# Attention and a tanh-shrink layer in one hand-ordered kernel: turns 96 to 574 of the first quarter in another order, 28 operations on another engine

## The chip, the cores and the metric

One Trainium2 core. It has TensorE (PE; matmuls into PSUM, with a weight load, PEld, ahead of each), VectorE (DVE), ScalarE (ACT), GpSimd (POOL) and SyncE (SP, which here only issues transfers). The metric is the device time of one execution in microseconds (us); the median of the runs is compared. PSUM has eight banks of 128 partitions by 2 KB; a matmul writes into them, and the other engines read the result out.

## The reference

Inputs q, k, v of [8 batches, 8 heads, 576 positions, 64] in float32 and two weights, w_in [512, 2048] and w_out [2048, 512]. The attention is a sum of two softmax attentions:

```python
# pooled: means over groups of 4 positions, result repeated 4 times
out_d = sm_attn(q_d, k_d, v_d);  out_up = np.repeat(out_d, 4, axis=2)
# local: only keys with |i - j| < 4
scores = np.where(np.abs(i - j) < 4, scale * q @ k.T, -1e9)
attn_out = out_up + softmax(scores) @ v
# the layer, on 4608 tokens of 512 values
x = attn_out.transpose(0, 2, 1, 3).reshape(4608, 512)
h = x @ w_in
out = (h - np.tanh(h)) @ w_out
```

## The kernel before, in words

**Pairs and batches.** Two heads make a pair, p = 0 to 31, four pairs make a batch, b = 0 to 7. A batch is one block of 576 tokens of the layer, so the attention of batch b is followed by the layer of block b, and attention for the next batch runs between the matmuls of the layer. The change lies in the stretch in which batch 0 and 1 (pairs 0 to 7) go through attention, the beginning of pair 8, and block 0's first layer.

**One pair, step by step, with lines.** SP issues the loads of q and k (tile st, 512 positions) and v (vst, 160 KB a head). The last 64 positions of all four pairs of a batch come as one tile sr, once a batch. Then:

- casts to bf16: qr for k and for q (L545, two operations), vw for v (L471), and once a batch rr from sr (L535). L535, L545 and L471 can each run on DVE, ACT or POOL.
- for pairs 0 to 7, PE transposes qr (L552) into PSUM, four transposes for k and four for q; kt (L557) and kq (L562) are copies of these out of PSUM, by ACT or DVE. Once a batch PE transposes rr (L575), ACT copies that to rT (L579), and the last columns of kt (L607) and kq (L612) are copied from rT. Later pairs use transposes by DMA that SP issues.
- the pooled k and q (qkd): for pairs 0 to 3, sums by PE (L659, L662) and a copy (L667); later, adds by DVE or POOL (L644 and L648 into half, L638 into qkd).
- scores in two parts, the first L696, the second L706 and L712. ACT takes the exp of the first part (L717) and of the second (L721 local, L725 pooled) into E; E is multiplied by the mask (L752, DVE or POOL).
- pooled v: PE (L502, from vw and the constant pick), copied into vp by ACT or DVE (L506). Its remainder, vpr, is built once a batch by three adds and multiplications (L433 vrs, L437 vrp, L440 vpr).
- the outs (L766), 18 matmuls of E with vw, vp and vpr; DVE takes the reciprocal r of the sums (L782) and multiplies (L784, tile ln).
- PE transposes ln back (L809, six transposes); od is a copy of the pooled part (L813 ACT, L815 DVE), and DVE joins both parts into xT, the layer's input (L802).

**The layer.** The first matmul of block 0 (L843) writes h for 128 of the 2048 columns in four steps, one for each pair's xT. ACT takes the tanh (L855) into u and DVE subtracts (L858) into gT. The second layer is L1137 and L1279; its results are copied to y (L1151 DVE or ACT). POOL issues the loads of the weights: w_in in four quarters (L452) and w_out in four (L456). Some filler matmuls of 128 by 512 (L1519), 24 in all, are placed by a string (FILL) where PE would otherwise be idle; they compute nothing that is used.

**The order is written out by hand.** The class Plan records 2263 operations with what each reads and writes, and emits them in the order of the string TURNS, two characters a turn. Each engine so gets its instructions in a fixed order, and an instruction that waits holds up all behind it on that engine. ENGINES has a letter for each operation that has a choice of engine (A for ACT, D for DVE, P for POOL). BANKS has a digit for each operation that opens PSUM banks; it can open them when everything that uses their earlier holder is done. BEHIND has pairs of operations: the first waits until the second is done, with the reason "shared port in this order". A wait from data, from a bank or from BEHIND becomes a semaphore wait.

```python
for i in turn:
    fn, deps, opens, names = self.ops[i]
    ...
    for name, sets in opens:
        c = self.place[name] = sets[int(next(seats))]
        ...
    if fn is not None:
        fn()
        ...
        if i in before:
            tc.add_manual_dep(seen[0], last[before[i]], ...)
```

## Time and profile before

| | before |
|---|---|
| median of 3 runs (us) | 308.03 (307.83 to 308.14) |
| profiled execution: its time, its span (us) | 311.41, 309.70 |
| TensorE, busy | 297.1 us, 96% |
| VectorE, busy | 266.9 us, 86% |
| ScalarE, busy | 224.3 us, 72% |
| GpSimd, busy | 157.1 us, 51% |
| granted clock of TensorE, mean | 0.992 |

The times are given by the slowest core, of which there is one here. The profile is of a single execution, whose time of 311.41 us stands beside the runs' median of 308.03; its span of 309.70 goes from its first recorded instruction to the last. In the profile, busy shares are of the span; a row of the timeline gives the start, the duration, the engine, the line and what the engine waited for before it (in brackets, with the time and the instruction that ended the wait). A row of windows gives busy time of each engine in a stretch, then the clock that was granted to TensorE (1.00 is full speed), the mean busy share of the DMA engines and what they moved in GB/s. In the page's rows of slices, each digit is a fortieth of the span, 7.7 us, in tenths.

Matmuls overlap: a row's duration includes a tail that runs on while the next matmul has started. What a step takes of TensorE when another follows at once is the distance from its start to the next start, called its slot here.

### The profile page before, as it was taken

The page shows a single profiled execution, that of the slowest core. Times are in us where ns is not written, and L with a number is a line of the kernel's source. Part 1 is how long each engine was busy: PE and PEld are TensorE (multiplying, and loading weights), DVE is VectorE, ACT ScalarE, POOL GpSimd, SP SyncE. Part 2 cuts the span into 40 slices and gives each one's busy share as a digit, 9 for nine tenths or more (in the row PEclk, how much of TensorE's full clock was granted, in tenths as well). Part 3 has the DMA queues.
Part 4 walks back from the last instruction along what each step waited for, and adds up shares of the span by engine and source line. Part 5 has one row for each costly group of instructions (what it writes and reads, how often), then busy time and mean ns, then how long its engine had stood idle before and what let it go on. Part 6 is the DMA issues. An engine that isn't in the chain of part 4 may idle for free.

```text
span 309.7 us, 8119 instructions
## 1 busy us (share of the span) xinstructions
PE 297.1 (96%) x3100; PEld 211.3 (68%) x3100; DVE 266.9 (86%) x493; ACT 224.3 (72%) x403; POOL 157.1 (51%) x213
## 2 busy tenths in 40 slices
PE   7777999999999999999999999999999999999994
PEld 3556555645487765784577755655988888889983
DVE  2674899688998988899998899899999999998783
ACT  3657678359887786888967888899867898875300
POOL 5325766108665546338874258547424264616550
PEclk9997999999999999999999999999999999999998
DMA  7999999989999999969999999999989526000333
GB/s 227 234 242 247 244 229 142 193 211 261 241 247 270 219 238 230 311 145 236 233 262 198 296 220 200 245 226 236 206 214 242 145 28 186 2 3 2 135 122 85
DMA packets 121191, 60.83 MB, mean 196 GB/s; under 512 B 88896, under 2 KB 119104, under 8 KB 121152
## 3 DMA queue, kind: packets, MB, share of 16 engines
q1 hardware_dynamic: 115968, 55.27, 76.9%
q0 software_dynamic: 4224, 4.19, 8.5%
q10 hardware_dynamic: 960, 0.85, 1.0%
q8 instruction: 24, 0.39, 0.5%
q14 instruction: 15, 0.12, 0.1%
HBM read 44.04 MB, written 9.44 MB: 173 GB/s over the span
## 4 chain that ended last, share of the span: by engine, by line
PE 87%; DMA 4%; SPq 3%; DVE 3%; issue 1%; ACT 1%; ACTq 0%
PE ps L1279 27%; PE ps L843 26%; PE ps L953 8%; PE ps L766 5%; PE ps L991 5%; PE ps L1137 4%; PE ps L696 3%; PE ps L1109 2%; SPq L411 2%; PE ps L1076 2%; DMA st<-in_k_dram 2%; DMA sr<-in_k_dram 2%; PE ps L809 1%; PE ps L712 1%; PE ps L502 1%; SPq L387 1%
## 5 line engine op out<-in xcount | busy, mean ns | idle before, releaser
L843 PE MATMUL ps<-xT,w_in_sb 128*128 128x512 bf16 x384 | 91.5, 379 | 0.0
L1279 PEld LDWEIGHTS <-gT 128*128 128x128 bf16 x672 | 64.5, 98 | 12.3
L858 DVE TENSOR_TENSOR gT<-ps,u 128x512 bf16<-128x512 f32 x96 | 64.2, 684 | 6.8 <-ACT u L855 5.6
L855 ACT ACTIVATE u<-ps 128x512 f32<-128x512 f32 x96 | 56.4, 599 | 16.3 <-PE ps L843 14.5
L843 PEld LDWEIGHTS <-w_in_sb 128*128 128x128 bf16 x384 | 35.3, 98 | 35.7
L545 POOL CAST qr<-st 128x512 bf16<-128x512 f32 x42 | 25.3, 613 | 42.2 <-DVE Tw L1188 15.5
L1279 PE MATMUL ps<-w_out_sb,gT 128*128 128x256 bf16 x336 | 43.4, 273 | 0.0
L1279 PE MATMUL ps<-Tw,gT 128*128 128x256 bf16 x336 | 42.5, 273 | 0.0
L717 ACT ACTIVATE E<-ps 128x912 bf16<-128x912 f32 x32 | 29.8, 932 | 6.3 <-PE ps L706 5.8
L784 DVE TENSOR_TENSOR ln<-ps,r 128x768 bf16<-128x768 f32 x32 | 30.6, 955 | 0.8
L623 ACT COPY kt<-kq 128x576 bf16<-128x576 bf16 x23 | 27.2, 1184 | 0.8 <-DMA kq<-qr 0.5
L766 PEld LDWEIGHTS <-E 128*128 128x128 bf16 x576 | 21.9, 98 | 6.0 <-DVE E L752 1.4
L752 DVE TENSOR_TENSOR E<-E,mask 128x1152 bf16<-128x1152 bf16 x31 | 23.5, 759 | 1.9 <-ACT E L721 1.6
L633 POOL TENSOR_TENSOR half<-kq 128x576 f32<-128x576 bf16 x16 | 20.5, 1278 | 8.4 <-ACT u L855 3.5
L725 ACT ACTIVATE E<-ps 128x576 bf16<-128x576 f32 x32 | 20.9, 654 | 1.4 <-PE ps L712 1.4
L766 PE MATMUL ps<-vw,E 128*128 128x65 bf16 x320 | 19.2, 194 | 1.0 <-DVE E L752 0.6
L638 POOL TENSOR_TENSOR qkd<-half 128x288 bf16<-128x288 f32 x21 | 16.7, 796 | 5.8 <-DVE r L782 2.0
L1214 DVE TENSOR_TENSOR gT<-gT 128x2048 bf16<-128x2048 bf16 x14 | 17.3, 1233 | 0.2
L1365 POOL TENSOR_TENSOR y<-y,keep 128x512 f32<-128x512 f32 x8 | 10.2, 1275 | 13.4 <-DVE E L752 4.8
L991 PE MATMUL ps<-xT,w_in_sb 128*128 128x128 bf16 x256 | 16.8, 219 | 0.0
L471 ACT CAST vw<-vst 128x640 bf16<-128x640 f32 x22 | 15.7, 729 | 1.1 <-DMA vst<-in_v_dram 1.1
L1301 ACT COPY y<-ps 128x512 f32<-128x512 f32 x19 | 11.1, 587 | 7.5 <-PE ps L1279 6.7
(183 smaller groups left out, 598.6 us busy)
## 6 DMA issues: line engine op xcount, KB each, us to landing
vst<-in_v_dram SPq DMA_DIRECT2D x56, 160.0 KB, 4.3
st<-in_q_dram SPq DMA_DIRECT2D x28, 256.0 KB, 4.1
st<-in_k_dram SPq DMA_DIRECT2D x28, 256.0 KB, 5.2
out_dram<-y SPq DMA_DIRECT2D x14, 512.0 KB, 4.2
v<-in_v_dram SPq DMA_DIRECT2D x20, 256.0 KB, 3.1
w_in_sb<-in_moe_w_in_dram POOLq DMA_DIRECT2D x4, 512.0 KB, 8.4
w_out_sb<-in_moe_w_out_dram POOLq DMA_DIRECT2D x4, 512.0 KB, 7.0
vr<-in_v_dram SPq DMA_DIRECT2D x8, 128.0 KB
```

What stands on the lines that cost most here:

```text
L545: (eng, ns, lambda dst=dst, src=src, fn=fn: fn(out=dst, in_=src), port)
L623: ("ACT", 1180, lambda: A.copy(out=ktv, in_=src), False),
L717: A.activation(out=E[s][:, :, E0:E0 + 456], in_=at(s1)[:, :, PS0:512], func=AF.Exp, scale=SCALE)
L752: eng.tensor_tensor(out=el, in0=el, in1=mask.unsqueeze(1).to_broadcast([128, 2, S]), op=ALU.mult)
L766: T.matmul(po[:, hh, 65 * n:65 * n + 65], E[s][:, hh, e:e + 128], vv, start=start, stop=stop)
L784: op("DVE", 960, lambda: V.tensor_tensor(out=ln[s].rearrange("p n (h d) -> p h n d", d=D), in0=blocks()[:, :, :, 0:64], in1=r[s].unsqueeze ...
L843: T.matmul(at(name)[:, 0, :], w_in_sb[:, dc, fc * 128:(fc + 1) * 128], xT[dc][:, c0:c0 + S].rearrange("p (c g) -> p c g", c=4)[:, :, 0:128 ...
L855: op("ACT", 600, lambda: A.activation(out=u[us], in_=at(name)[:, 0, :], func=AF.Tanh), reads=[("hd", kb, fc)], writes=[("u", us)], uses=[n ...
L858: op("DVE", 690, lambda: V.tensor_tensor(out=gT[g][:, fc, :], in0=at(name)[:, 0, :], in1=u[us], op=ALU.subtract), reads=[("hd", kb, fc), ( ...
L953: T.matmul(at(("hz", kb, G, bk))[:, 0, 256 * x:256 * x + 256], left(k, x), right(k), start=(first and x == 0 and k == 0), stop=(k == 1), s ...
L991: T.matmul(at(name)[:, 0, 128 * f:128 * f + 128], w_in_sb[:, dc, (f0 + f) * 128:(f0 + f) * 128 + 128], xT[dc].rearrange("p (b c g) -> p b ...
L1279: T.matmul(dst, left[:, f, 128 * j:128 * j + 128], right[:, f, :], start=(first and e == 0 and f == 0 and (j == 0 or apart)), stop=(e == 1 ...
```

## The change

Four strings change. In TURNS, the turns 96 to 574 are a permutation of what they were; everything before and after them stays. In ENGINES, 28 letters change. BANKS and BEHIND follow the new order. The operations, their code, FILL and the order of SP's transfers are the same.

What goes to another engine: the cast of v for pair 0 (ACT to POOL); the copies of vp for pairs 1, 3, 5, 6 (ACT to DVE); the casts of qr (pair 4: k ACT to DVE, q DVE to ACT; pair 7 k ACT to POOL; pair 8 k DVE to POOL); the copies of kt and kq (pair 3 kq, pair 4 kt and kq, pair 7 kq DVE to ACT; pair 5 kt ACT to DVE); the last columns of kt (pairs 2, 3, 5 DVE to ACT; pair 7 ACT to DVE) and of kq (pair 8 ACT to DVE); the copies of qkd for pairs 2 and 3 (ACT to DVE) and its add for pair 8 (DVE to POOL); od (pairs 2 and 7 DVE to ACT, pair 4 ACT to DVE); vrs of batch 1 (DVE to POOL); the mask of pair 5 (DVE to POOL); one copy of y (ACT to DVE).

What changes place on an engine, of that which matters most in the first 35 us: on ACT, two of pair 3's three exps (L717, L721) stood behind the cast of rr for batch 1 and stand ahead of it now, while the third (L725) stays behind it; on PE, the q transposes and sums of pair 3 move ahead of pair 0's outs, pair 1's outs ahead of pair 4's k transposes, and the back-transposes of pair 0 and the pool matmul of pair 2 stand directly ahead of the transposes of rr; on DVE, the joins of pairs 0 and 1 and the mask of pair 3 stand ahead of the reciprocal for pair 2. In BEHIND, ten waits that have both ends in this stretch go, eight come and three stay. With the new ones, the cast of v for pair 0 waits for the mask of pair 0, that for pair 1 for the mask of pair 1, and the half sum of pair 6 for the mask of pair 4; the issue of the last w_out quarter waits for a cast of pair 8.

The diff, with the parts of the strings that change:

```diff
     TURNS = (
...
-        "0k0l1x2Z091V2I2J0y2T082G2H1z1D2V291E2W0o0p261F1d1e2U1X1l1m212X27201n1o2z1Y2b1Z0z391p1q2a"
-        "0q0r2d282c2n2o1r1G2e311h1i1s2f2p2q2g2A2K2L322Y1t3A3B2B2O2y5H2C3C3D302D2P3G5I332E1a353E0s"
-        "0t2M2N5J34362v2h2F373N3O5K5L5P2i1b5e5f383F0u0v5M5S2w5N2r2s2j5O5Q3H5U5R3I3J5v662Q2k683K5B"
...
+        "0k0l1x2Z091V2I2J270y292G1z260o1d0p2a2T2U1E1D1l2V2W08391F2z1X280z212Y3A1n1o1p0q2n1h2p1Y1Z"
+        "202b2d2c1q2e2g2q1r1s2A0r2B2X3B3C3D2C2D3E1a1G2f2K1t2H5H1b1c2O2P2E5I0s2M2F1e2y33311i3G2v2w"
+        "5J5K3N5e0t3432371m2L3F5N302h2o5L5M3H352i2j2k36385S5P0u2r2s5Q5R5U3I3J3K3L3M2Q2l2m633d3e3j"
...
     ENGINES = (
-        "APADDADAADPPDDPPDDADDDDAPPDADDAADDDPDDDDDAADDADAADDDAAADDDPPAPPPAADAPPPDAAPAPADADPPPDDAA"
-        "APADAAPPPDAAPPDDAAPPPDDAAAADDPDADDAADDDDAPPPDDPPDAAAPPAAPPDDAAPPPAAPPDDPPADDADDADAAPPDAP"
+        "PPADDADAADPPDDPPDDADDDDDPPDADAAADDDPDDDAAADDADDADAAAAADDDPPPAPPPDAAAPPPDDDPAPADADPPPPDDA"
+        "PPAADAPPPDAAPPPDDAPPPDADAAADDPDADDAADPDDAPPPDDPPDAAAPPAAPPDDAAPPPAAPPDDPPADDADDADAAPPDAP"
...
     BANKS = (
-        "0123453012067016731120212706021330112130022310312010302101013121001113020110023303011200"
-        "2131010210231012301102321001203101010110123031002311201210012130120131010102030210302321"
+        "0123453012067016022310210543322012033151200301101210301201331320011033221100321023011210"
+        "2031023210231012301102321001203101010110123031002311201210012130120131010102030210302321"
...
     BEHIND = (
-        "0211 1H12 1D1V 0z20 1t2f 5I30 5Q5N 635B 5w5W 6562 6c2x 6d6A 5u6i AACD ABCH AmAF AnAL DxC"
-        "J F8CZ FfFD DFFn MUFt GAGb IrJ6 JNK7 MZJs NBKu OELA LqNn ODLO O7OQ QoNy RYOp RZP8 T3Rd S"
-        "WPQ PiSi TVTU TaRk TPUO TnUY TmTO WZU7 WeWc WfVu XWX6 XcXP Z5Yy ZqZ4 ZpZH"
+        "0211 1H12 AmAF AnAL DxCJ F8CZ FfFD DFFn MUFt GAGb IrJ6 JNK7 MZJs NBKu OELA LqNn ODLO O7O"
+        "Q QoNy RYOp RZP8 T3Rd SWPQ PiSi TVTU TaRk TPUO TnUY TmTO WZU7 WeWc WfVu XWX6 XcXP Z5Yy Z"
+        "qZ4 ZpZH 0y1V 0z28 1t2f 5P3F 6b5W 6c2x 6U6Z 3b73 9g9f AACF ABCH"
```

More of the change, by code (lines that the diff above doesn't have):

```diff
@@ new lines @@
+        "5J5K3N5e0t3432371m2L3F5N302h2o5L5M3H352i2j2k36385S5P0u2r2s5Q5R5U3I3J3K3L3M2Q2l2m633d3e3j"
+        "5B5O665C645D5w3p3k3q3l3m0w3P3f683n3o653v3w3g5v3h3x3i0v5E2t5F5k5T5x3r3s3y5V0x5X2N5z603t3u"
+        "4147485y494A424361673z694B626B5W4D4E4F4G404H4J6b2x4K4L4M4C444I5Y6e45466g4N5Z5a4P6c6d4Q4V"
+        "4W4X4O3T3V4Y4Z4a5g4R4S4T3O6T6V6W5b5c5d4b4c4h4i3Q4j5f3X3R6A5h4U4d4e4f6Z3U6U7A5s5t2u5G4k4l"
+        "4m4g4n4o4p4q4r4s4t4u6X6Y6a6C6D4z50515l727D7F555657523Y6E6Q6R4v6F53547B7C6G585m6H593W4w4x"
@@ new lines @@
+        "7f88893S3Z5u715n7E7I4y6f6h7G5A8d7473768e96976y6z6K6L6I5i5q3b7g3c6i6j8E7H8F9C6k6l3a6m9D77"
+        "7J7K7L8K8L6n6o758j789f7M7N6p7l9g7m7r7s7O9a799h9i8Q8R8S7x7y9I7X9J9k5rCC6J9Z7z9j9l6w5o6M6u"
+        "6q6s9b6O7P9v9wCG7b7c8k8p5p6S6r7Y7ZCB8q9c6N8v9t9u5j9T7d8w9U7V7WCD9OCF8x9P7R7S7eAA9m9W6v7h"
+        "9V9X6x9Y7i7a6t7n9QCH7o7j9nAB7p7k7t6P70ACAD809d9o9p849eAGAd7uA1A27qAe9q9zA0AH7vA79r817T7Q"
+        "7U9sCEA8BD857w82ELEMAIAh9x9y86838AAgAJ8B878GAiAjCI8H8C8MAEAM8VAFATAU8I8NAVAW8DAm8WAKAbAc"
```

9 lines of the change are left out of this document (removed).

## The prediction

> **What bounds the kernel now.** First the page: its total, its busy line and two of its rows by slices.
>
> ```profile
> span 309.7 us, 8119 instructions
> ...
> PE 297.1 (96%) x3100; PEld 211.3 (68%) x3100; DVE 266.9 (86%) x493; ACT 224.3 (72%) x403; POOL 157.1 (51%) x213
> ...
> PE   7777999999999999999999999999999999999994
> ...
> PEclk9997999999999999999999999999999999999998
> ```
>
> TensorE (PE) is busy for 297.1 of 309.7 us. What it lacks lies in the first four slices (7.7 us each), and so does the dip of its clock. The windows view gives that stage in stretches of 5 us.
>
> ```profile
> core 0: us, PE busy (x) PEld busy (x) DVE busy (x) ACT busy (x) POOL busy (x), PEclk, DMA share, GB/s
> ...
> 20.00:25.00 5.00, 2.52 (x46) 1.80 (x45) 2.78 (x7) 2.50 (x6) 1.52 (x4) 0.97 1.11 232
> 25.00:30.00 5.00, 4.54 (x55) 3.87 (x54) 1.89 (x9) 3.63 (x10) 2.49 (x4) 0.68 1.18 266
> 30.00:35.00 5.00, 4.56 (x62) 2.98 (x63) 4.93 (x14) 3.47 (x7) 4.37 (x7) 1.00 1.20 225
> 35.00:40.00 5.00, 5.00 (x43) 2.63 (x42) 3.88 (x9) 3.34 (x8) 2.96 (x4) 1.00 1.04 247
> ```
>
> From 35 us on PE is full (5.00 of 5.00; nines in the slices). So a reordering that adds no PE work can gain only ahead of that, and what it gains there moves the rest of the program as a whole. The worst stretch has 2.52 of 5.00, the next a granted clock of 0.68. PE's waits, its timeline and that of ScalarE (ACT) show the cause of the first.
>
> ```profile
> PE ps L575 <- ACT E L717: 2.5, 1, 2.5
> ```
>
> ```profile
> 19.22 0.45 PE L502 MATMUL ps<-vw,pick 128*128 128x128 bf16 x5 [1.07 <-POOL vw L471]
> 19.50 0.39 PE L552 MATMUL ps<-ident,qr 128*128 128x128 bf16 x4
> ...
> 19.94 0.32 PE L766 MATMUL ps<-vw,E 128*128 128x65 bf16 x5
> ...
> 20.49 0.38 PE L1519 MATMUL ps<-lT 128*128 128x512 bf16 x1
> 20.80 0.38 PE L696 MATMUL ps<-kq,kt 64*128 64x112 bf16 x8
> 21.12 0.46 PE L502 MATMUL ps<-vw,pick 128*128 128x128 bf16 x5
> ...
> 22.02 0.50 PE L809 MATMUL ps<-ident,ln 128*128 128x128 bf16 x6
> 25.01 0.59 PE L575 MATMUL ps<-ident,rr 128*128 128x128 bf16 x4 [2.49 <-ACT E L717]
> ...
> 28.31 0.39 PE L552 MATMUL ps<-ident,qr 128*128 128x128 bf16 x4
> 28.53 0.38 PE L1519 MATMUL ps<-lT 128*128 128x512 bf16 x1
> ...
> 30.02 0.33 PE L766 MATMUL ps<-vw,E 128*128 128x65 bf16 x5 [0.47 <-DVE E L752]
> ...
> 32.14 0.51 PE L809 MATMUL ps<-ident,ln 128*128 128x128 bf16 x6 [0.42 <-DVE ln L784]
> ...
> 33.16 0.38 PE L843 MATMUL ps<-xT,w_in_sb 128*128 128x512 bf16 x1
> ```
>
> ```profile
> 23.51 0.62 ACT L535 CAST rr<-sr 128x512 bf16<-128x512 f32 x1 [2.50 <-DMA sr<-in_k_dram]
> 24.04 0.92 ACT L717 ACTIVATE E<-ps 128x912 bf16<-128x912 f32 x1
> ```
>
> The transposes L575 open a PSUM bank that pair 3's scores hold until their exp (L717) has read them, and wait 2.49 us for it. The scores (20.80) were done at about 21.1. But in ACT's order the exp stands behind the cast of batch 1's remainder rr, and that one waits 2.50 us for its DMA. ACT idles with work ready behind the head of its queue. Then the clock halves, as the windows of 3.41 us around it show:
>
> ```profile
> 17.93:21.34 3.41, 2.33 (x47) 1.78 (x44) 3.08 (x6) 2.06 (x6) 1.60 (x2) 1.00 1.02 279
> 21.34:24.75 3.41, 1.18 (x18) 0.80 (x16) 1.23 (x3) 1.24 (x2) 1.27 (x2) 1.00 1.15 212
> 24.75:28.16 3.41, 3.15 (x37) 3.15 (x37) 1.12 (x5) 2.61 (x7) 2.69 (x4) 0.50 1.16 287
> ```
>
> The stretch ahead of the drop has PE busy for 1.18 of 3.41 (35%); the one before it, at 2.33 (68%), led to none.
>
> **The change, part by part.** Turns 96 to 574 of the 2263 are permuted, 28 operations change engine, some banks and hand-written waits change. PE's 3100 matmuls stay, SyncE's transfers keep their order. I walked the new order by hand with the durations of this trace, every dependency and each bank's earlier holder; the sum goes by slots of PE, from start to start.
>
> *To 19.2 us: nothing.* The pool matmul at 19.22 waits for the same landing of v, behind a cast on GpSimd (POOL). POOL takes pair 0's cast of v from ACT and ends it 0.4 us later, but the 1.07 us of that wait cover it; without them it would cost up to 0.4.
>
> *19.2 to 25 us: the exp ahead of the cast.* The exp L717 of pair 3 and the shorter L721 now stand ahead of the rr cast on ACT and run in its idle time, at about 21 to 22.2. The cast still starts with its DMA at 23.51 and ends 0.62 later at 24.13, with the bank long free: L575 at about 24.17 instead of 25.01. Meanwhile PE does the back-transposes of pair 0 inside the hole, which came after it before; pair 2's pool matmul (21.12) only changes place. Slots without work: before 2.66 (six transposes take 0.33 from 22.02, then nothing until 25.01); after 0.38 for ln of pair 1 and 1.19 for the cast, together 1.57. The wait isn't gone: the DMA is next late.
>
> *25 to 28.3 us: the clock.* From 25.01 to 28.31 PE does six steps in 3.30 us: four transposes three times, six transposes, a pool matmul, one pair's outs. At full rate the rows above give 0.22 for four transposes (28.31 to 28.53), so 0.33 for six, 0.28 for a pool matmul (19.22 to 19.50) and 0.55 for outs (19.94 to 20.49): 1.82. The half clock costs 1.48. After the change I count 2.25 us of PE work in 21.34 to 24.75, 66%, close to the 68% without a drop. I take no drop. If it comes all the same, half-rate slots laid under the new order lose about 0.75, since its other waits cover some of them: the bounds are 0 and 0.75, and 66% is nearer to the end at 0.
>
> A rule speaks against this. The Trainium skill, "TensorE: Matmul & The Clock Gate", section "Part 4: PE-mode transpose", says that a transpose doesn't count as PE-busy for the clock gate as a matmul does. Without transposes the share in 21.34 to 24.75 would be, by my estimate, 24% before and 28% after, so by that rule the clock falls again and the sum is that of rival B; no stretch of this trace tells the two counts apart.
>
> *28.3 to 33.2 us: one set of waits for another.* Before, PE stood for 0.64 in slots ahead of 30.02 (pair 3's mask on VectorE, DVE) and 0.61 ahead of 32.14 (ln). In the new order these end, and I find 0.33 at pair 2's outs (a vp copy that goes to DVE), 0.34 at pair 3's (its mask, now from about 25.99), 0.36 and 0.14 at the back-transposes of pairs 2 and 3 (ln), 0.15 at scores 4 (a kq copy that goes to ACT) and 0.80 at scores 5 (their filler waits for pair 2's join on DVE): 2.12. The other casts and copies that change engine (kt, kq, od, qkd, qr) run beside PE's work in this walk; where one ends a wait it is named.
>
> *Sum.* Slots lost after 19.22: before 2.66 + 1.48 + 0.64 + 0.61 = 5.39, after 1.57 + 2.12 = 3.69; gain 1.70. By equal work: the long run of L843 goes on from 31.37 in the walk, with three of its matmuls done (0.65) and 0.56 of pair 4's scores and pool matmul still to do; before, at 33.16, it was the other way round, so 33.16 + 0.65 − 0.56 − 31.37 = 1.88. I take **1.8**.
>
> *35 to 76 us: held.* From turn 575 (about 76 us) the order is the old one. Until there the tight engine is POOL, which also issues the weight loads.
>
> ```profile
> 25.36 0.75 POOL L452 DMA_DIRECT2D w_in_sb<-in_moe_w_in_dram  x1
> ...
> 35.95 0.80 POOL L452 DMA_DIRECT2D w_in_sb<-in_moe_w_in_dram  x1
> ```
>
> ```profile
> w_in_sb<-in_moe_w_in_dram POOLq DMA_DIRECT2D x4, 512.0 KB, 8.4
> w_out_sb<-in_moe_w_out_dram POOLq DMA_DIRECT2D x4, 512.0 KB, 7.0
> ```
>
> With 8.4 and 7.0 us from issue to landing the second w_in quarter, issued about 25.2, comes 1.6 us before its matmul, the last (34.85) 1.1 before, the third w_out part (48.65) 1.1 before. POOL takes pair 5's mask from DVE, and behind it stands the cast for pair 7's q transposes:
>
> ```profile
> L752 POOL TENSOR_TENSOR E<-E,mask 128x1152 bf16<-128x1152 bf16 x1 | 2.4, 2372 | 0.0
> L545 POOL CAST qr<-st 128x512 bf16<-128x512 f32 x42 | 25.3, 613 | 42.2 <-DVE Tw L1188 15.5 <-DVE gT L1214 11.0 <-DVE qr L545 4.6
> L644 POOL TENSOR_TENSOR half<-kt 128x288 f32<-128x288 bf16 x4 | 2.8, 702 | 4.3 <-ACT kt L607 3.9 <-DVE vrs L433 0.3
> L648 POOL TENSOR_TENSOR half<-kq 128x288 f32<-128x288 bf16 x4 | 2.9, 728 | 2.5 <-DVE kt L607 2.2 <-ACT kq L612 0.3
> L638 POOL TENSOR_TENSOR qkd<-half 128x288 bf16<-128x288 f32 x21 | 16.7, 796 | 5.8 <-DVE r L782 2.0 <-DVE gT L1214 2.0 <-DVE E L752 0.8
> ```
>
> Mask 42.3 to 44.7, cast to 45.3, transposes wanted at 45.7: 0.4 us of slack, no cost. The DVE time that goes free (0.75) hides nothing that PE waits for there.
>
> **The rivals.** *B, the clock falls all the same*: for it, the busy share stays under 68%; against, it nearly doubles. 1.8 − 0.75, gain about 1.1: 306.9. *C, the drop is no part of the timed runs*: the profiled run took 311.41 us against a median of 308.03, and one trace can't show that each run drops there. The gain is then 1.8 − 1.48, about 0.3 to 0.4: 307.6. The Trainium skill, "TensorE: Matmul & The Clock Gate", section "What's actually happening", calls the gate's window free-running, so that the place of a drop shifts by run; one trace can't show that.
>
> *D, slower: POOL becomes the bound at 42 to 46 us.* From the half sums of pair 6 to that cast it has 0.70 + 0.73 + 0.80 + 0.61 + 2.37 + 0.61 = 5.8 us of work, beside DVE all the time. One POOL operation here shows what that can do:
>
> ```profile
> L440 POOL TENSOR_TENSOR vpr<-vrp,hsel x7: 1056/1060/1603, 14.6 to 212.0; 128x520 bf16<-128x520 bf16 x7
> ```
>
> 1603 ns against 1060 is a stretch of 1.5. If all six stretch so, the transposes come 2.9 − 0.4 = 2.5 us late, on a PE that is full: 1.8 gained, 2.5 lost, 308.7. It turns to slower from a stretch of about 1.38. Against: 42 casts (25.3 us) average 613 ns next to a busy DVE.
>
> *E, the shift is given back*: the front moves 1.8 us earlier and a transfer that keeps its time (a weight load, or SyncE's loads in an unchanged order) takes most of it back: about 308.0. Against: the slack of 1.1 and more above.
>
> **How the numbers follow.** The sum is made on the profiled execution (span 309.7, run 311.41). What goes is time of PE in the span, so it is carried as it is to the median: 308.03 − 1.8 = **306.2**. Chances: the forecast 0.47, B 0.20, C 0.10, D 0.15, E 0.08. A measurement of this kernel can tell about 0.2%, 0.62 us, from no change. Faster is the forecast, B and a little of C: 0.69; the same is the rest of C and E: 0.16; slower is D: 0.15. The range goes from 305.5 (a third of the new waits' 2.12 doesn't come) to 308.1, which takes in B, C and E and leaves out D.
>
> **What would show it.** In the profile after: L575 near 24.2 with a wait of about 1.2 on rr's cast, no longer on L717; ACT's exp of pair 3 at about 21, ahead of that cast; a granted clock of 1.00 in 20 to 30 us (below that: B); the first L843 at about 29.4 and the long run from 31.4; 5.00 of 5.00 from 35 us on; the mask on POOL at about 42.3 for 2.4 us. It would be wrong if the wait at 24 us went to another engine for its whole length, if the waits from 30 us on took over 4 us, or if PE stood at 45 us behind POOL.

## The result, and the profile after

| | before | after |
|---|---|---|
| median (us) | 308.53 (14 runs, 307.83 to 310.60) | 310.68 (14 runs, 309.14 to 315.04) |
| ratio after / before, 95% interval | | 1.0067 (1.0044 to 1.0089) |
| profiled execution: its time, its span (us) | 311.41, 309.70 | 310.71, 309.0 |
| granted clock of TensorE in it, mean | 0.992 | 1.00 |

The change makes the kernel **slower**, by 0.67% or 2.1 us. The prediction was 306.2 us, with a range from 305.5 to 308.1, and gave 0.15 to this sign. It is wrong in sign and in range. Yet the profile after has a span that is 0.7 us *shorter* than the profile before. That contradiction is the key to the case, and the first experiment opens it. First the page of the changed kernel:

```profile
span 309.0 us, 8101 instructions
...
PE 296.2 (96%) x3091; PEld 210.0 (68%) x3100; DVE 266.3 (86%) x491; ACT 223.1 (72%) x399; POOL 162.2 (52%) x219
...
PE   8878999799999999999999999999999999999995
...
PEclk9999999999999999999999999999999999999999
```

The clock's dip is gone and the first slices are fuller (8, 8, 7, 8 for 7, 7, 7, 7). But a 7 has appeared in the eighth slice, 54 to 62 us, where the kernel before had a 9. (The 3091 matmuls are 3100 of which nine left no record.) The windows of the changed kernel, with the columns as in the prediction's:

```profile
20.00:25.00 5.00, 3.99 (x71) 3.17 (x68) 4.90 (x14) 4.24 (x10) 2.52 (x4) 1.00 1.16 242
25.00:30.00 5.00, 3.72 (x55) 2.24 (x55) 3.63 (x10) 2.62 (x6) 4.14 (x6) 1.00 1.18 251
...
55.00:60.00 5.00, 4.47 (x45) 2.40 (x43) 2.29 (x5) 0.56 (x2) 0.00 (x0) 1.00 1.61 143
60.00:65.00 5.00, 3.17 (x25) 1.65 (x27) 3.51 (x9) 2.62 (x4) 0.79 (x1) 1.00 1.17 266
```

PE has 3.99 of 5.00 at 20 to 25 us (2.52 in the profile before) at full clock. At 60 to 65 us, where the prediction says 5.00, it has 3.17. PE's timeline of the changed kernel at the places that matter:

```profile
17.38 0.23 PE L706 MATMUL ps<-kq,kt 64*128 64x120 bf16 x2 [0.40 <-DVE qkd L667]
...
21.05 0.84 PE L809 MATMUL ps<-ident,ln 128*128 128x128 bf16 x12 [0.61 <-DVE ln L784]
21.73 0.45 PE L502 MATMUL ps<-vw,pick 128*128 128x128 bf16 x5
22.12 0.40 PE L575 MATMUL ps<-ident,rr 128*128 128x128 bf16 x4
...
26.44 0.51 PE L809 MATMUL ps<-ident,ln 128*128 128x128 bf16 x6 [0.18 <-DVE ln L784]
...
27.92 0.81 PE L843 MATMUL ps<-xT,w_in_sb 128*128 128x512 bf16 x3
29.40 0.39 PE L1519 MATMUL ps<-lT 128*128 128x512 bf16 x1 [0.67 <-DVE xT L802]
...
30.04 2.33 PE L843 MATMUL ps<-xT,w_in_sb 128*128 128x512 bf16 x10
...
57.58 1.89 PE L1137 MATMUL ps<-w_out_sb,gT 128*128 128x512 bf16 x8
61.67 0.38 PE L696 MATMUL ps<-kq,kt 64*128 64x112 bf16 x8 [2.20 <-ACT kt L623]
```

L575 comes at 22.12 and waits for nothing. New waits are there too (0.40 for a pooled copy, 0.61 and 0.18 for ln, 0.67 for pair 2's join). And at 61.67 pair 8's scores wait 2.20 us for a copy of kt, in a stretch that the prediction held to be full.

### The profile page after: what moved, and what is told of

It is laid out like the page before. It is cut to its first block, busy times and chain, and to the rows that moved or that the text cites. A ratio compares the mean times of both kernels' runs of the same rounds, so it can differ in the third digit from the quotient of the medians.

```text
span 309.0 us, 8101 instructions
## 1 busy us (share of the span) xinstructions
PE 296.2 (96%) x3091; PEld 210.0 (68%) x3100; DVE 266.3 (86%) x491; ACT 223.1 (72%) x399; POOL 162.2 (52%) x219
## 4 chain that ended last, share of the span: by engine, by line
PE 83%; DMA 6%; DVE 5%; SPq 3%; issue 1%; ACT 0%; ACTq 0%; DVEq 0%
PE ps L1279 27%; PE ps L843 26%; PE ps L953 8%; PE ps L766 5%; PE ps L991 5%; DMA kq<-qr 3%; PE ps L696 3%; PE ps L1137 2%; PE ps L1109 2%; PE ps L1076 2%; SPq L411 2%; DMA sr<-in_q_dram 2%; DMA sr<-in_k_dram 1%; PE ps L712 1%; DVE xT L802 1%; SPq L387 1%
## 5 line engine op out<-in xcount | busy, mean ns | idle before, releaser
L843 PE MATMUL ps<-xT,w_in_sb 128*128 128x512 bf16 x384 | 92.0, 379 | 0.0
L1279 PEld LDWEIGHTS <-gT 128*128 128x128 bf16 x672 | 64.5, 98 | 12.3
L843 PEld LDWEIGHTS <-w_in_sb 128*128 128x128 bf16 x384 | 35.2, 98 | 35.3
L545 POOL CAST qr<-st 128x512 bf16<-128x512 f32 x43 | 26.3, 622 | 33.7 <-DVE gT L1214 11.4
L717 ACT ACTIVATE E<-ps 128x912 bf16<-128x912 f32 x32 | 29.9, 934 | 10.3 <-PE ps L706 4.8
L623 ACT COPY kt<-kq 128x576 bf16<-128x576 bf16 x23 | 27.2, 1183 | 2.7 <-DMA kq<-qr 2.4
L638 POOL TENSOR_TENSOR qkd<-half 128x288 bf16<-128x288 f32 x22 | 17.5, 797 | 12.9 <-DVE half L633 9.2
L725 ACT ACTIVATE E<-ps 128x576 bf16<-128x576 f32 x32 | 21.0, 657 | 1.3 <-DVE gT L858 0.7
L1214 DVE TENSOR_TENSOR gT<-gT 128x2048 bf16<-128x2048 bf16 x14 | 17.3, 1233 | 0.2
L1365 POOL TENSOR_TENSOR y<-y,keep 128x512 f32<-128x512 f32 x8 | 10.2, 1276 | 13.4 <-DVE E L752 4.8
L766 PE MATMUL ps<-vpr,E 128*128 128x65 bf16 x128 | 16.3, 194 | 0.0
```

Of the source, the lines that this page charges most:

```text
L545: (eng, ns, lambda dst=dst, src=src, fn=fn: fn(out=dst, in_=src), port)
L623: ("ACT", 1180, lambda: A.copy(out=ktv, in_=src), False),
L717: A.activation(out=E[s][:, :, E0:E0 + 456], in_=at(s1)[:, :, PS0:512], func=AF.Exp, scale=SCALE)
L766: T.matmul(po[:, hh, 65 * n:65 * n + 65], E[s][:, hh, e:e + 128], vv, start=start, stop=stop)
L843: T.matmul(at(name)[:, 0, :], w_in_sb[:, dc, fc * 128:(fc + 1) * 128], xT[dc][:, c0:c0 + S].rearrange("p (c g) -> p c g", c=4)[:, :, 0:128 ...
L1279: T.matmul(dst, left[:, f, 128 * j:128 * j + 128], right[:, f, :], start=(first and e == 0 and f == 0 and (j == 0 or apart)), stop=(e == 1 ...
```

## The experiments

### 1. The kernel before, profiled again

No edit: the kernel before as it stands, for a second profile.

> The kernel before once more, unchanged, for a second profile: the first one took 311.41 us where the timed runs have a median of 308.5. Theory 1 (the first profile's hole at 22.5 to 25 us and its half clock are no part of most runs): about 308.5 us, rr's cast waits for its DMA less than 2.5 us by 1 us or more, granted clock 1.00 throughout. Theory 2 (hole and drop are in every run): the wait of L575 again 2.5 us, clock 0.5 for 3.4 us from about 24.8, and a time near 311.

It took 308.14 us, with a span of 306.4: close to the kernel's median (308.28 in 25 runs on the same chip), and 3.27 us less than the 311.41 of the profile on which the prediction was built. Its rows for the place of the hole, the window first, then ACT's timeline and PE's:

```profile
21.34:24.75 3.41, 2.53 (x47) 2.25 (x47) 1.65 (x6) 3.06 (x7) 2.28 (x4) 1.00 1.20 216
```

```profile
21.66 0.62 ACT L535 CAST rr<-sr 128x512 bf16<-128x512 f32 x1 [0.88 <-DMA sr<-in_k_dram]
```

```profile
23.16 0.38 PE L575 MATMUL ps<-ident,rr 128*128 128x128 bf16 x4 [0.88 <-ACT E L717]
...
29.87 0.38 PE L843 MATMUL ps<-xT,w_in_sb 128*128 128x512 bf16 x1
```

The same program: rr's load ends its cast's wait at 21.66 instead of 23.51, L575 waits 0.88 us instead of 2.49, PE is busy for 2.53 of the 3.41 us instead of 1.18, and the clock stays at 1.00. The L843 that stood at 33.16 stands at 29.87, 3.29 earlier, and from there on the two executions keep that distance to the end. Of the 3.29, the hole is 1.61 and the half clock behind it 1.46; 0.24 had come before. What the change was credited with removing is, in this execution, mostly not there to remove.

Three kernels of the later experiments have the same front (rear_new, rear_300, b_w3late). In their profiles L575 waits 1.53, 1.12 and 1.61 us, and only in rear_300 does a half clock follow at once. So the hole varies from run to run, and the 2.49 us of the first profile are the largest of five.

The times alone gave a reason to doubt it: 311.41 stood beside a median of 308.03 with a range of 0.3. The prediction cites the two numbers, draws rival C from them, and takes off the clock alone (1.48). Most of the hole belonged to the same excess.

### 2. Each half of the change, cut at turn 360

front_new runs the changed kernel's turns up to 360 (about 44 us) and what is left in the order of before; rear_new the reverse. In the string of turns:

```diff
front_new:  TURNS = after[:360]  + the rest in the order of before
rear_new:   TURNS = before[:360] + the rest in the order of after
```

> The first 360 turns of the changed order (to about 46 us), then the order of before for what is left. Theory 1 (the loss of the change lies behind 46 us, where pair 8's scores and the last w_out quarter stand too early for their transfers): not slower than before, 307.0 to 308.6 us. Theory 2 (the loss lies in the front, where GpSimd took over the mask of pair 5 and casts): about 310.5, as the whole change.

> The first 360 turns of before, then the changed order for what is left. Theory 1: slower than before by about 2 us, 310 to 311, with PE standing ahead of pair 8's scores (L696) near 60 us. Theory 2: 308.5, as before.

front_new: 310.97 us, ratio 1.0082 (1.0059 to 1.0106). rear_new: 311.59 us, 1.0097 (1.0065 to 1.013). Each half loses at least as much as the whole, which neither theory had for both, so the two don't add up. Their waits show one reason: front_new has a wait of its own behind the cut, 1.5 us of PE at pair 6's second scores for ln, rear_new one of 0.9 us (L843 for gT). An order that is cut pays at the seam. Cut at turn 300 instead (experiment 7) it is no better. What holds from these two: there is no large gain in the front which the rear would hide, and rear_new, with the front of before, shows the transfers at 53 to 62 us of the changed kernel again (the last w_out quarter takes 9.3 us and PE waits 0.54 us for it, see experiment 4).

### 3. The exp ahead of the cast, alone

The edit for which the prediction expects the gain, on the kernel before, on ACT:

```diff
+L717 Activation E_114<-ps 128x2x456
 L535 TensorCopy rr_80<-sr_78 128x2x4x64
-L717 Activation E_114<-ps 128x2x456
 L725 Activation E_114<-ps 128x2x2x144
```

> The kernel before with one instruction moved: pair 3's exp L717 ahead of the cast of rr on ACT. Theory 1 (the step that the prediction built on works, but in most runs the hole is 0.9 to 1.5 us and no half clock follows): L575 waits for rr's cast and no longer for L717, gain 0.3 to 0.9 us, so 307.4 to 308.0. Theory 2 (as the prediction sized it): gain 1.5 to 2.3 us, 306.0 to 306.8. Theory 3: the gain is swallowed by the next wait before 35 us, under 0.2.

> The kernel before with pair 3's exp L717 ahead of the cast of rr, once more. If its gain is real: 0.994 to 0.999 of before again, and hardly a run with a granted clock of 0.995 or less (none of 12 in the first try, 17 of 101 runs of before). If the first result was a draw: 0.999 to 1.003 and such runs as often as before.

The first run gave 308.07 us, ratio 0.9969 (0.9945 to 0.9994), the repeat 308.78 us, 1.0007 (0.998 to 1.0033). The gain isn't confirmed. The mechanism works, as PE's row shows, with no wait left:

```profile
22.62 0.40 PE L575 MATMUL ps<-ident,rr 128*128 128x128 bf16 x4
```

Together the two intervals leave it anything from a gain of 0.55% to a loss of 0.33%. The traces fit a small gain: in the profiles of before's front without a drop of the clock the wait was 0.88 to 1.61 us, and what comes next takes part of it (pair 3's outs wait 0.80 us for their mask here, 0.48 in the second profile of before).

Two wider forms were tried. b_exp3 moves L721 up along with L717; b_exp2 also moves pair 3's mask on DVE ahead of pair 2's reciprocal, as the change does:

```diff
 ACT (both)
+L717 Activation E_114<-ps 128x2x456
+L721 Activation E_114<-ps 128x2x120
 L535 TensorCopy rr_80<-sr_78 128x2x4x64
 DVE (b_exp2 only)
+L752 TensorTensor E_114<-E_114,mask 128x2x576
 L782 Reciprocal r_115<-ps 128x12
 L815 TensorCopy od_121<-ps 128x144
-L752 TensorTensor E_114<-E_114,mask 128x2x576
```

> The kernel before with pair 3's exps L717 and L721 both ahead of the cast of rr on ACT, and on DVE the mask of pair 3 ahead of the reciprocal for pair 2. If the wait of pair 3's outs for its mask (0.8 us with L717 alone moved) goes as well: 307.4 to 307.9, faster than before by 0.2 to 0.4% and than L717 alone. If the mask ahead of the reciprocal only delays pair 2: 308.0 to 308.4.

> The kernel before with L717 and L721 ahead of the cast, the mask of pair 3 where it was. If b_exp2 lost by its mask: as with L717 alone, 307.6 to 308.2. If it lost by L721 ahead of the cast (0.4 us of ACT that come before the cast in runs where the load lands early): 308.2 to 309.2, with half-clock runs as in b_exp2 (4 of 12).

b_exp2: 309.36 us, 1.0022 (0.9995 to 1.0049). b_exp3: 308.41 us, 0.9995 (0.9971 to 1.0018). Neither can be told from no change, and b_exp2 is slower than its expectation had it either way. The front's main idea, taken alone, brings nothing measurable.

### 4. The wait at 61.67: the order, or two transfers beside each other

Where does pair 8's kt come from? SP transposes rT (L590) and kq (L596) by DMA, once the casts of pair 8 are done; ACT then copies kt (L623). SP, POOL and ACT of the changed kernel, then SP and ACT of before in its second profile:

```profile
49.65 1.32 SPq L590 DMA_TRANSPOSE rT<-rr  x1
51.19 1.27 SPq L596 DMA_TRANSPOSE kq<-qr  x1
```

```profile
51.42 0.74 POOL L456 DMA_DIRECT2D w_out_sb<-in_moe_w_out_dram  x1 [1.80 <-DVE qr L545]
```

```profile
60.45 1.17 ACT L623 COPY kt<-kq 128x576 bf16<-128x576 bf16 x1 [2.38 <-DMA kq<-qr]
```

```profile
51.84 1.32 SPq L590 DMA_TRANSPOSE rT<-rr  x1
54.00 1.23 SPq L596 DMA_TRANSPOSE kq<-qr  x1
```

```profile
57.78 1.17 ACT L623 COPY kt<-kq 128x576 bf16<-128x576 bf16 x1 [0.48 <-DMA kq<-qr]
```

The changed kernel issues the transposes **2.8 us earlier** (51.19 for 54.00) and has kt **2.7 us later** (60.45 for 57.78). From the end of the issue to the copy it is 8.0 us for 2.55. What else is in flight: the change puts pair 8's casts ahead of the last w_out quarter, and by BEHIND (3b73) POOL waits 1.80 us for one of them, so that this load of 512 KB goes out at 51.42, right behind the transposes. The DMA view, for the stretch in which it alone of the weight loads is issued (last column: issue to landing in us), first of the changed kernel and then of before:

```profile
w_out_sb<-in_moe_w_out_dram POOLq DMA_DIRECT2D x1, 512.0 KB, 10.2
```

```profile
w_out_sb<-in_moe_w_out_dram POOLq DMA_DIRECT2D x1, 512.0 KB, 7.3
```

It too takes 2.9 us longer, and lands at 61.66. In before it went out at 48.80 and had landed at 56.10, and for the first 5 us it had no transpose of kq beside it. The windows of before's second profile at that place have PE full:

```profile
55.00:60.00 5.00, 5.00 (x45) 2.75 (x43) 3.69 (x10) 1.60 (x2) 0.00 (x0) 1.00 1.11 229
60.00:65.00 5.00, 5.00 (x37) 2.27 (x35) 3.90 (x9) 3.11 (x6) 0.00 (x0) 1.00 0.99 214
```

The DMA engines were busier in the changed kernel in 55 to 60 us (mean share 1.61 for 1.11) and moved less (143 for 229 GB/s). A rival reading is that only PE's order is at fault: the scores of pair 8 stand ahead of ten w_out matmuls (L1137) that come first in before. a_mm2_first puts those ten ahead again:

```diff
 PE
+L1137 Matmult ps<-w_out_sb,gT_123 128x512      (ten, with their weight loads)
 L696 Matmult ps<-kq_94,kt_96 128x112
 ...
-L1137 Matmult ps<-w_out_sb,gT_123 128x512      (the same ten)
```

> The changed kernel with ten matmuls of the second layer that need no late transfer (2.2 us of PE) moved ahead of pair 8's scores on PE; nothing else moves. Theory 1: the wait of 2.2 us ahead of L696 and of the last w_out quarter shrinks to under 0.5, and the time falls by about 2 us to 308.5. Theory 2: the wait only moves to another place, the time stays at 310 to 311.

310.47 us, ratio 1.0053 (1.003 to 1.0077). PE's row and ACT's:

```profile
63.96 0.38 PE L696 MATMUL ps<-kq,kt 64*128 64x112 bf16 x8 [1.35 <-ACT kt L623]
```

```profile
62.74 1.17 ACT L623 COPY kt<-kq 128x576 bf16<-128x576 bf16 x1 [3.70 <-DMA kq<-qr]
```

The wait is still there, as kt is now ready at 62.74: transposes issued by 53.45 land 9.2 us later, and the w_out quarter beside them takes 12.3 us. So not the order alone. The transfers are what is late, and how late differs from run to run.

### 5. The two transfers apart, and, on the kernel before, brought together

a_w3early takes out the wait that holds the quarter, so that it goes out directly behind the one before it; a_w3both does this and puts the ten matmuls first. b_w3late puts the same wait into the kernel before: the quarter goes behind pair 8's cast. There that cast comes later, so the quarter goes out 9.2 us later than in before's second profile (57.97 for 48.80), where the change delays it by 2.6 (51.42).

```diff
 POOL, a_w3early and a_w3both, against after (BEHIND loses 3b73)
-L456 DMACopy w_out_sb<-in_moe_w_out_dram 128x4x512
+L456 DMACopy w_out_sb<-in_moe_w_out_dram 128x4x512 x2
 L471 TensorCopy vw_91<-gT_124 128x10x64
 L535 TensorCopy rr_79<-sr_77 128x2x4x64
-L456 DMACopy w_out_sb<-in_moe_w_out_dram 128x4x512

 POOL, b_w3late, against before (BEHIND gains 3b73)
-L456 DMACopy w_out_sb<-in_moe_w_out_dram 128x4x512
 L471 TensorCopy vw_91<-gT_124 128x10x64
 L535 TensorCopy rr_79<-sr_77 128x2x4x64
+L456 DMACopy w_out_sb<-in_moe_w_out_dram 128x4x512
```

> The changed kernel with the issue of the last w_out quarter directly behind the third, so ahead of the DMA transposes of pair 8, and no wait on pair 8's cast. Theory A (the transposes and that load delay each other, because it is issued just behind them): the quarter lands near 57 instead of 61.7, kq near 58 instead of 60.4, the wait ahead of L696 falls from 2.2 to under 0.7, time 308.3 to 309.2. Theory B (the transposes are that slow anyway, pair 8's scores simply stand too early on PE): kq still at 60 or later, the wait stays over 1.5, time 310 to 310.7.

> The same, and ten matmuls of the second layer ahead of pair 8's scores, as tried alone before. Theory A: no wait left at 58 to 64 us, 307.8 to 308.6, level with before. Theory B: also near 308.5, since then the scores stand later and the quarter lands in time; a time over 309.5 speaks against both.

> The kernel before with the last w_out quarter issued behind pair 8's cast for the q transposes, as the change has it (about 54 instead of 48.8 us). Theory A: kq of pair 8 lands 2 us or more later than 57.7 and the quarter takes 10 us instead of 7.3; PE waits for it ahead of the second layer's matmuls that need it, time 310 to 313. Theory B: kq lands as before at 57.5 to 58.5; the quarter lands at 61.5 and costs 1 to 2 us, 309.5 to 310.5.

| | median (us) | ratio (95%) | kq: end of issue to landing | w_out quarter: issue to landing | PE waits at its use |
|---|---|---|---|---|---|
| before (2nd profile) | 308.53 | | 55.23 to 57.7: 2.5 | 48.80 to 56.10: 7.3 | none |
| after | 310.68 | 1.0067 (1.0044 to 1.0089) | 52.47 to 60.4: 7.9 | 51.42 to 61.66: 10.2 | 2.20, kt |
| a_mm2_first | 310.47 | 1.0053 (1.003 to 1.0077) | 53.45 to 62.7: 9.2 | 52.32 to 64.58: 12.3 | 1.35, kt |
| a_w3early | 310.31 | 1.0055 (1.0029 to 1.0082) | 55.11 to 60.0: 4.9 | 49.78 to 58.49: 8.7 | 0.41, kt |
| a_w3both | 310.62 | 1.0067 (1.0042 to 1.0092) | 56.65 to 61.7: 5.0 | 50.11 to 60.19: 10.1 | none |
| b_w3late | 313.09 | 1.0126 (1.0084 to 1.0168) | 58.97 to 64.4: 5.4 | 57.97 to 66.58: 8.6 | 2.9, w_out |

The rows' medians come from different chips; each ratio is against the kernel before on the same chip, and compares. In b_w3late one load and one wait of the change, on the kernel before, cost 1.26%, 3.9 us, and its waits of PE name the load (the profile is of an execution that took 316.23, so its size isn't read as an ordinary one):

```profile
PE ps L1137 <- DMA w_out_sb<-in_moe_w_out_dram: 2.9, 1, 2.9
```

This is a harsher delay than the change's, and PE waits for the load itself and not for kt. So it shows that the place of this load matters, and that kq takes 5.4 us instead of 2.5 when only the load is moved; it doesn't show what the transfers cost in the changed kernel.

In the other direction a_w3early has a wait of 0.41 us instead of 2.20, but its ratio falls only from 1.0067 to 1.0055, which is within the intervals. Part of the shorter wait is that PE comes to it 1.42 us later in this profile. Counted from the start of the eight L1137 ahead of the scores, which take PE about 1.8 us, kt is ready after 4.04 us in the changed kernel and after 2.24 in a_w3early. Its transposes still have the load beside them for their first 3.4 us. a_w3both has no wait at this place and still the whole loss, and its expectation had called a time over 309.5 us evidence against both theories. So the waits at this place alone don't account for the medians. In the front a_w3early has a wait of 1.39 us that stood at 0.40 in the profile after. That one is the next experiment.

### 6. A cast at the head of VectorE's queue, and both repairs together

The wait at 17.38 in the profile after (L706 for the pooled copy qkd of pair 3) is one of the change's own. DVE's timeline of a_w3early, and then PE's, show where it comes from:

```profile
17.30 0.43 DVE L545 CAST qr<-Tw 128x512 bf16<-128x512 f32 x1 [1.47 <-DMA Tw<-in_k_dram]
```

```profile
18.81 0.23 PE L706 MATMUL ps<-kq,kt 64*128 64x120 bf16 x2 [1.39 <-DVE qkd L667]
```

The change gives pair 4's cast of k to DVE, where it waits for its load with the mask of pair 1 and the copy L667, both ready, behind it. This wait of PE was 0.34, 0.40, 0.57, 1.30, 1.30, 1.34 and 1.39 us in seven profiles of kernels with this front. a_kcast puts the cast behind the two; a_late_tr leaves it and goes on with the rear: on top of a_w3early it holds pair 8's casts back (rr on POOL behind the mask of pair 6, q on DVE behind two masks), so that the transposes come later, as in before; a_best is both.

```diff
 DVE, a_kcast
+L752 TensorTensor E_114<-E_114,mask 128x2x576
+L667 TensorCopy qkd_100<-ps 128x2x144
 L545 TensorCopy qr_92<-Tw_134 128x2x4x64
-L752 TensorTensor E_114<-E_114,mask 128x2x576
-L667 TensorCopy qkd_100<-ps 128x2x144

 DVE, a_late_tr (besides a_w3early's edit; BEHIND gains 716i)
+L752 TensorTensor E_113<-E_113,mask 128x2x576
+L752 TensorTensor E_114<-E_114,mask 128x2x576
 L545 TensorCopy qr_92<-st_73 128x2x4x64
-L752 TensorTensor E_113<-E_113,mask 128x2x576
-L752 TensorTensor E_114<-E_114,mask 128x2x576
```

> The changed kernel with one cast moved on DVE: pair 4's k cast, whose load comes late, stands behind the mask of pair 1 and the qkd copy of pair 3 instead of ahead of them. Theory A (in the runs so far it held DVE for 0.4 to 1.5 us and so PE ahead of L706 for 0.3 to 1.4): L706's wait on L667 goes, PE has lost 0.3 to 1 us less by 40 us, time 309.7 to 310.4. Theory B (the next wait takes its place): PE's loss by 40 us stays at 15.7 to 17.2 us, time 310.4 to 311.

> The changed kernel with the last w_out quarter issued directly behind the third, and the two casts for pair 8's DMA transposes held back behind the masks of pairs 6 and 7, so that the transposes are issued 2 to 3 us later. Theory A (transposes and weight load delay each other when they run together): kq lands within 3 us of its issue, at 56 to 58, earlier than the 60.0 and 60.4 of the earlier issues; no wait at 58 to 64; time 308.2 to 309.2. Theory B (the transposes need until 60 whatever is beside them, or a later issue only makes them later): kq at 60 or later, time 310 to 311.

> Both edits together. Theory A on both points: 307.6 to 308.6, level with before or a little faster. If the front of the change still costs as much as it gains, not below 308.

| | median (us) | ratio to before (95%) | kq: end of issue to landing | PE waits |
|---|---|---|---|---|
| a_kcast | 309.89 | 1.0057 (1.0031 to 1.0083) | 52.85 to 59.5: 6.6 | L706: gone; kt: 1.19 |
| a_late_tr | 309.30 | 1.0044 (1.0024 to 1.0063) | 58.00 to 60.6: 2.6 | L706: 1.34; none after 36 us |
| a_best | 309.54 | 1.0045 (1.0023 to 1.0066) | 58.27 to 60.6: 2.3 | L706: gone; none of over 0.3 after 36 us |

SP, ACT and PE in a_late_tr:

```profile
56.74 1.26 SPq L596 DMA_TRANSPOSE kq<-qr  x1
```

```profile
60.64 1.18 ACT L623 COPY kt<-kq 128x576 bf16<-128x576 bf16 x1 [0.32 <-DMA kq<-qr]
```

```profile
59.84 1.89 PE L1137 MATMUL ps<-w_out_sb,gT 128*128 128x512 bf16 x8
61.87 0.38 PE L696 MATMUL ps<-kq,kt 64*128 64x112 bf16 x8
```

Issued 5.55 us later than in the changed kernel, the transposes arrive 0.2 us later, and no wait of PE is listed. This profile runs 2.26 us behind that of the changed kernel, by a drop of the clock and the wait in the front: the eight L1137 start at 59.84 for 57.58, and the third w_out quarter goes out at 49.79 for 47.54. Counted from the eight L1137, kt is ready after 1.98 us here, 1.74 in a_best and 4.04 in the changed kernel, so the repair does its work on the transfers. Most of it was there in a_w3early (2.24), by the earlier load: in both, kq lands 1.5 to 1.6 us behind the load (59.98 behind 58.49, 60.56 behind 58.95), so that a later issue mainly shortens the time from issue to landing, 4.9 to 2.6. The expectations weren't met: a_late_tr's had kq at 56 to 58 us and a time of 308.2 to 309.2, a_best's 307.6 to 308.6 if both edits worked. a_kcast's time is in its range, but its gain on the changed kernel (1.0057 for 1.0067) can't be told from none.

By the ratios a_late_tr takes back a third of the loss (0.44% is left of 0.67%), with intervals that overlap. That PE stands 2.20 us for late transfers in the changed kernel is shown by its trace; that they are the cause of the slower median is likely only. Neither a_late_tr nor a_best beats the kernel before.

### 7. Cut at turn 300

```diff
front_300:  TURNS = after[:300]  + the rest in the order of before
rear_300:   TURNS = before[:300] + the rest in the order of after
```

> The first 300 turns of the change (to about 40 us), then the order of before. The cut at 360 tried earlier brought a wait of its own at 44 us; this one is to show the front alone. Theory F (in ordinary runs the new waits of the front, above all at about 30 us for pair 2's join, cost more than the old ones that they replace): 308.7 to 309.4 us, PE's loss by 40 us 0.5 to 1 above before's ordinary 15.1 to 15.7. Theory G (the front is worth nothing either way): 308.0 to 308.6. The prediction's front would give 306.4.

> The first 300 turns of before, then the change's order. If the rest of the loss of the change lies there, with its transposes issued beside the last w_out quarter: 309.5 to 310.5 us, kq landing more than 4 us after its issue and the quarter taking over 8.5 us. If the rear costs only where the front has moved: under 309.

front_300: 310.83 us, ratio 1.006 (1.004 to 1.0079). rear_300: 310.54 us, 1.0057 (1.0032 to 1.0083). front_300 is slower than either of its theories had it. They have their own waits behind the cut again (0.7 us, and 0.4 and 0.3), and the front of front_300 has the wait of L706 at 1.30. In rear_300 the last w_out quarter takes 7.9 us, less than expected, and PE waits neither for it nor for kt; so at least in an order that is cut a loss of this size comes without the wait at 61.67. The share of front and rear can't be had by cutting; it is read from the traces, in the next part.

## Why the prediction was wrong, point by point

The size of each part, from the traces: for each instruction of PE, how much later the next one starts than its work needs, summed over the stretch. The sums are mine; the nine matmuls without a record make those of the changed kernel uncertain by some tenths.

| PE time lost (us) | up to 40 us | 40 to 75 us |
|---|---|---|
| before, the first profile | 18.06 | 0.73 |
| before, the second profile | 15.10 | 0.51 |
| after | about 15.3 | 3.11 |
| a_late_tr (with a drop of the clock) | about 17.3 | 1.26 |
| a_best (with a drop of the clock) | about 17.6 | 1.03 |

Against the first profile, the front of the changed kernel gains some 2.8 us. Against the second, it gains nothing (the same sums over the other profiles without a drop there give about 15.7 for before's front in rear_new, and 15.3 to 16.6 for the change's front in seven); the rear loses 2.4 and 2.6. 0.2 + 2.6 = 2.8, near the difference of the spans (309.0 − 306.4 = 2.6) and of the medians (2.15).

**The basis: the step that failed first.** "What goes is time of PE in the span, so it is carried as it is to the median: 308.03 − 1.8". The span had 3.3 us that the median doesn't have, in just the place where the 1.8 was to come from. Carried rightly, the 1.8 should have been set against a hole of 0.88 to 1.61 us and a clock that in most runs doesn't fall: rival C's place, with more taken off than C took. C had the drop as no part of the timed runs, the hole as a part of all.

**To 19.2 us: nothing.** Roughly right for the cast of v, which the step names. It missed the cast of k of pair 4, which is on its list of operations that "run beside PE's work in this walk": on DVE, it waits for its load at the head of the queue, and PE stands for 0.34 to 1.39 us at L706. The step fixed the time of a load by one trace and so saw no wait; the load's landing varies by more than a microsecond.

**19.2 to 25 us.** The mechanism is right: the exp stands ahead of the cast, and L575 no longer waits for it. The times aren't: L575 was given at 24.17, 1.19 us late behind a cast that waits for its load until 23.51. In the profile after it is at 22.12 without a wait. ACT's timeline shows why: the exp at 20.36, and the cast behind it and L721, with no wait for its load:

```profile
20.36 0.93 ACT L717 ACTIVATE E<-ps 128x912 bf16<-128x912 f32 x1 [1.39 <-PE ps L696]
...
21.44 0.62 ACT L535 CAST rr<-sr 128x512 bf16<-128x512 f32 x1
```

The wait for ln is 0.61, where 0.38 was given.

**25 to 28.3 us: the clock.** The clock of the profiled execution stays at 1.00, as forecast. That is no effect of the change: it stays there in before's second profile too. Over all runs, a mean clock of 0.995 or less (one stretch of 3.41 us at half rate lowers it by 1.71 / 309 = 0.0055) was granted in 19 of 124 runs of before and in 8 of 14 of after. So rival B's condition came about in over half of the runs, but it doesn't explain the loss: the medians of after's runs with and without it are 310.44 and 310.93. In a_late_tr, four runs with it lie at 310.30 to 310.91 and the eight others at 308.94 to 309.42, so there it costs about 1.5 us, which the step had at 1.48.

The step's reading of shares ("66%, close to the 68% without a drop") lacks one thing, the place of the stretch. Half-rate stretches lie on a grid of 3.41 us: in b_w3late's profile they begin at 31.84 and 65.98 us, ten lengths apart, and in before's first profile the clock halves at 24.75 and, with the work done, at 308.06, 83 lengths later. Where the grid lies in the traces without a drop can be had from their record of the clock, which begins and ends on it (in a_w3early at 5.92 and 309.70, 89 lengths). The rows show a stretch of a_w3early off the grid, its two neighbours on it, two of a_late_tr on it, and two of the changed kernel, the first on the grid, the second off it:

```profile
16.80:20.21 3.41, 1.27 (x22) 0.85 (x20) 2.76 (x6) 2.01 (x5) 1.60 (x2) 1.00 0.97 260
16.15:19.57 3.42, 1.82 (x41) 1.50 (x40) 2.24 (x5) 2.02 (x7) 1.11 (x2) 1.00 1.04 270
19.57:22.98 3.41, 2.26 (x46) 1.71 (x45) 2.29 (x6) 2.02 (x6) 0.49 (x1) 1.00 1.08 229
```

```profile
17.46:20.87 3.41, 1.57 (x31) 1.24 (x30) 2.48 (x6) 1.99 (x4) 1.60 (x2) 1.00 0.91 253
20.87:24.28 3.41, 3.08 (x36) 2.53 (x34) 2.38 (x5) 2.22 (x4) 0.84 (x2) 0.50 1.15 196
```

```profile
26.04:29.46 3.42, 2.33 (x28) 1.26 (x26) 2.63 (x8) 2.09 (x5) 2.96 (x6) 1.00 1.20 235
58.26:61.67 3.41, 1.21 (x6) 0.37 (x5) 1.18 (x4) 1.17 (x1) 0.27 (x1) 1.00 1.14 256
```

The 37% of a_w3early lie across two stretches of the grid with 53 and 66%, and the clock stays. The 46% of a_late_tr are one stretch of it, and the next is at half rate. Over the 18 profiles, up to the last 3 us of each, all six half-rate stretches follow one with PE busy for 35 to 55%; of the other some 1560 stretches only three are that low (52, 53 and 53%). So the share went with the fall here, up to this overlap; what one trace can't give in advance is where the stretches will lie in the next run. The Trainium skill, "TensorE: Matmul & The Clock Gate", section "What's actually happening", has the gate's window run freely, not from the kernel's start; the traces agree, as the five in which the clock falls have five different grids from the start of the span (24.75, 20.87, 23.10, 15.56 and 31.84 us leave 0.86, 0.39, 2.62, 1.91 and 1.12 when whole lengths are taken off). Its other rule, in "Part 4: PE-mode transpose", that transposes don't count as PE-busy in the same way, isn't borne out: without them the changed kernel's stretch from 26.04 has 37% instead of 68%, and no half rate follows, while one does behind the 46% of a_late_tr, which hold no transpose.

**28.3 to 33.2 us: one set of waits for another.** Right in kind. The largest, pair 2's join, is there at 0.67 (0.80 given), ln at 0.18 (0.36 and 0.14 given). The first L843 comes at 27.92, the long run at 30.04, where 29.4 and 31.4 were given: both 1.4 to 1.5 us early, as the hole was smaller in this execution too.

**35 to 76 us: held. The step that failed with the most time in it.** It priced the weight loads by 8.4 and 7.0 us from issue to landing, gave the third w_out part 1.1 us, followed POOL's chain, and left out two things that the change moves: the last w_out quarter, whose new wait is in the list of the change ("the issue of the last w_out quarter waits for a cast of pair 8"), and pair 8's transposes by DMA, which wait for casts that moved earlier. It took the duration of a transfer as given. In fact the load took 10.2 us and the transposes 7.9 instead of 2.5, and PE stands for 2.20 us in the profiled execution. A new wait on the issue of a transfer moves that transfer beside others, and this one wasn't looked at. Rival E had the idea of a transfer that takes the gain back, with another transfer (a load that keeps its time) and a price that ended at no change.

**Rival D**, POOL as the bound at 42 to 46 us, was the only one on the slower side, and it isn't what happened. The mask on POOL takes 2.38 us, as forecast; the cast behind it (43.58) is held for 0.17 only, and PE has no wait there.

```profile
41.03 2.38 POOL L752 TENSOR_TENSOR E<-E,mask 128x1152 bf16<-128x1152 bf16 x1
43.58 0.61 POOL L545 CAST qr<-Tw 128x512 bf16<-128x512 f32 x1 [0.17 <-DVE kt L607]
```

**What stays open.** a_late_tr and a_best still lose 0.44 and 0.45%, about 1.4 us, though PE waits for little in them after 36 us. The table above gives 0.5 to 0.8 of it to the rear, in small pieces; the front's part isn't pinned down. Why the clock falls more often with the change isn't shown either. The waits of PE are a candidate: that of 2.20 us leaves PE busy for 35% of 58.26 to 61.67 in the changed kernel, that of L706 for 37% of 16.80 to 20.21 in a_w3early, and the grid decides whether such a stretch counts, while in before's second profile no 3.41 us between 8 and 72 us have under 67%. But a_kcast, without the wait of L706, has 4 drops in 12 runs, as many as a_late_tr; a_w3both, without the wait for kt, has 7; and a_best, without either, has 1.

## What to carry to other kernels

Compare the profiled execution's time with the median before anything is built on its idle time: if it is longer by as much as the hole that you want to close, most of the hole may not be in the median, and a second profile can show it. A change that holds a transfer back, or brings one forward, has to be priced with all other transfers in flight at that time, as durations from the old order don't hold in the new one. An instruction that waits for a load holds up the ready work behind it; moved behind that work, it took PE's wait out of the trace here (a_kcast), with no gain in the median that could be told.

## What the runs showed of the hardware that was not expected

- DMA transposes from SP land late beside a 512 KB weight load from POOL's queue. In the 12 profiles in which the load is issued first, kq lands 1.5 to 1.8 us behind the load's landing, though its own issue had ended 0.1 to 3.5 us before that. Where the load is issued just behind the start of the transposes, kq takes 5.4 to 9.2 us from the end of its issue (five profiles; 2.5 in before's second profile). The load takes 7.9 to 12.3 us there and 6.5 to 10.1 where it is issued first, so what it loses itself isn't settled. Which resource they share isn't shown; in 55 to 60 us the mean DMA share went up (1.61 for 1.11) while the bytes moved went down (143 for 229 GB/s).
- The same program had its hole at 23 us at 2.49 us in one execution and at 0.88 in another, by a load that landed 1.85 us earlier, and of these two the clock dropped to half for 3.4 us only behind the first.
- The clock of TensorE falls for one stretch of a grid of 3.41 us whose place differs from run to run, and all six falls came behind a stretch of the grid with PE busy for 55% or less.
